# Attention's value products, two units to a PSUM bank in place of one, with 18 buffers for the turned numerators in place of 12

## The chip, the cores and the metric

The kernel runs on one core of one Trainium2 chip. The metric is the device time of one execution in microseconds (us). A difference of 0.5% of it is some 3.3 us.

## What is computed

Clustered attention on `q`, `k`, `v` of shape (2, 8, 768, 64), then two mixing layers (`_moe_ref` and `_moe2_ref`) on the (2, 768, 512) result. The change lies in the attention:

```python
scores = scale * np.matmul(q, k.transpose(0, 1, 3, 2))
scores = np.where(mask, scores, -1000000000.0)
scores = scores - np.max(scores, axis=-1, keepdims=True)
attn = np.exp(scores)
attn = attn / (np.sum(attn, axis=-1, keepdims=True) + 1e-09)
return np.matmul(attn, v)
```

## The kernel before

The attention is cut into 48 **units**, one per batch b, head h and third u of the queries (256 of 768). A name such as `s062` means batch 0, head 6, query tile 2 (a unit has the query tiles 2u and 2u+1); two heads are a **pair**, six units. Each unit passes three stages on PE (TensorE):

- `scores` (L381): for each of its two query tiles, four matmuls of 384 columns (L398, L399) into a tile `s` of two PSUM banks. Pool `ps_s` has two such tiles. DVE (VectorE) takes the negated row maximum `nm` (L401), ACT (ScalarE) the exponential `e` with its row sums (L403). Only then may the tile be written again, by the scores two query tiles later.
- `turn` (L410): twelve transposes of `e` (L418) into three PSUM tiles `t` of one bank (pool `ps_t`, three tiles, which the masks' products and `natural` use too). Each is copied to an SBUF tile `p`: two of the three by ACT (L421), the third by DVE (L423). There are `PB` buffers of tag `p`.
- `values` (L427): the products of the turned numerators with `v` (L439). Even and odd key tiles go to the two 64-column halves of the array (`tile_position=(0, r)`), into one half of the PSUM bank `o` (pool `ps_o`, one bank). Then ACT copies the upper 64 partitions to `tmp` (L446), and DVE adds the lower 64 to it, into `xt` (L448).

The loop over the units (L486) is skewed: step n traces the scores of unit n, the transposes of unit n-1 and the values of unit n-2 (`SKEW`). `values` takes a list of `GROUP` units: all their products first, then all their evacuations.

```python
group.append((n - SKEW, prs.pop(n - SKEW), ops[b, h][4]))
if len(group) == GROUP:
    with tc.issue_after(marks["turn"].ins):
        values(group)
    group = []
```

Once a pair, masks for a later pair are made (products `sim` into 32-column strips of the array at L247, a product `pp` at L271, the rest on DVE), and `natural` (L452) transposes a finished pair (L461) and divides by the row sums (DVE, L463). The order of each engine's instructions is set by the compiler's list scheduler from this program; at run time each engine runs its list in order and waits on semaphores. After the attention, from about 240 us on, the mixing layers run on PE nearly without a pause; weights are loaded and split for them on ACT, DVE and POOL (L104 to L117, L81 to L87).

Of the kernel before, what the change touches and what calls it, by code (L numbers as in the profile page):

```python
# [25 lines left out]

KINDS = "AAV"

GROUP = 1
PB = 12  # L30
RAW = 4
HL = 4

# [17 lines left out]
def tile_model(ctx: ExitStack, tc: tile.TileContext, qT, kT, v, cent, w1, w2, wc1, wc2, wth, wri, wch, out):  # L51
# [110 lines left out]
    with ExitStack() as actx:  # L162
# [247 lines left out]
        def turn(b, h, u, es):  # L410

            pr = []
            for j in range(NT // 2):
                ps = ps_t.tile([P, 2, 256], F32, tag="t", name=f"t{b}{h}{u}{j}")
                for i in range(2):
                    for a in range(2):
                        kt = 2 * j + a
                        marks["turn"] = nc.tensor.transpose(ps[:, a, i * P : i * P + P], es[i][:, kt * P : kt * P + P], ident)  # L418
                p = ap.tile([P, 2, 256], F32, tag="p", bufs=PB, name=f"p{b}{h}{u}{j}")
                if KINDS[j] == "A":  # L420
# [65 lines left out]
        for n in range(len(units) + SKEW):  # L486
# [42 lines left out]
            if 0 <= n - SKEW:  # L529
                b, h, u = units[n - SKEW]  # L530
# [3 lines that stand above are left out]
# [273 lines left out]
```

## Time and profile before

| what | value |
|---|---|
| time, median of 3 runs | 660.72 us (660.63 to 663.01) |
| the profiled execution: its time | 661.38 us |
| its span | 659.5 us (1.9 us lie around it) |
| granted TensorE clock, mean | 0.995 of full |
| busy: PE, PE's weight loads, DVE, ACT, POOL | 98%, 78%, 61%, 52%, 39% |

A profile row gives the line, the engine, the operation, the tiles (out<-in) and how often. In a timeline the first number is the start in us, the second the time covered; matmuls are pipelined, so that the distance from one start to the next is what a matmul costs, not its length. "[0.62 <-ACT e L403]" says that the engine sat idle for 0.62 us and that L403 of ACT ended it. A 32-bit matmul of L439 stands twice in the trace, so that a unit's six products are twelve records.

### The profile page before, as it was taken

How to read it: one execution, taken by the hardware profiler on the slowest of the kernel's cores; microseconds unless marked ns; L12 is line 12 of the kernel's file. 1: busy time of each engine (PE TensorE's matmuls, PEld its weight loads, DVE VectorE, ACT ScalarE, POOL GpSimd, SP SyncE). 2: the span in 40 equal slices, each digit the busy share in tenths (PEclk: the TensorE clock that was granted, in tenths of full speed). 3: DMA queues.
4: the chain of work that ended last, by engine and by line, in shares of the span. 5: the costliest groups of instructions: out<-in, count | busy, mean ns of one | idle time of the engine just before them, and what ended most of it. 6: DMA issues, size and time to landing. Idle time of an engine off the chain costs nothing. (4 is left out here: it accounts for less than half of the span.)

```text
span 659.5 us, 9798 instructions
## 1 busy us (share of the span) xinstructions
PE 645.3 (98%) x3591; PEld 517.3 (78%) x3591; DVE 399.9 (61%) x649; ACT 344.5 (52%) x653; POOL 258.4 (39%) x231
## 2 busy tenths in 40 slices
PE   7999999999999999999999999999999999999998
PEld 4777777777777767878888878888888888888886
DVE  6777878687777777466655432537577875431212
ACT  6676766776768763256544520427486954320000
POOL 7230303255031131138786520602467698541000
PEclk8999999999999999999999999999999999999999
DMA  8554656454454221013444321210022224410001
GB/s 297 158 125 110 169 122 159 102 135 101 109 132 108 66 73 64 24 64 128 133 155 128 97 64 32 68 62 0 1 64 65 72 88 144 125 50 33 16 33 48
DMA packets 24207, 61.42 MB, mean 93 GB/s; under 512 B 4256, under 2 KB 7520, under 8 KB 24160
## 3 DMA queue, kind: packets, MB, share of 16 engines
q1 hardware_dynamic: 24160, 60.80, 32.8%
q8 instruction: 28, 0.46, 0.3%
q14 instruction: 19, 0.16, 0.1%
HBM read 39.65 MB, written 3.15 MB: 65 GB/s over the span
## 5 line engine op out<-in xcount | busy, mean ns | idle before, releaser
L401 DVE TENSOR_REDUCE nm<-s 128x1 f32<-128x768 f32 x96 | 90.5, 950 | 20.1 <-PE s L399 19.2
L403 ACT ACTIVATE e<-s,nm 128x768 f32<-128x768 f32 x96 | 86.6, 905 | 29.4 <-DVE nm L401 28.1
L418 PE MATMUL t<-ident,e 128*128 128x128 f32 x576 | 81.2, 276 | 0.6 <-ACT p L421 0.5
L418 PEld LDWEIGHTS t<-ident,e 128*128 128x128 f32 x576 | 67.0, 141 | 16.3 <-issue 9.4
L398 PE MATMUL s<-k,qh 128*128 128x384 f32 x188 | 72.3, 385 | 2.4 <-ACT e L403 2.3
L439 PE MATMUL o<-p,vs 128*64 128x256 f32 x564 | 71.2, 388 | 0.0
L399 PE MATMUL s<-k,q 128*128 128x384 f32 x192 | 65.7, 345 | 1.9 <-DVE q L280 1.9
L421 ACT ACTIVATE p<-t 128x512 f32<-128x512 f32 x96 | 52.2, 594 | 25.8 <-PE t L418 25.4
L127 PE MATMUL r<-ul,c_h 128*128 128x512 f32 x144 | 56.5, 396 | 0.4 <-DVE ul L91 0.4
L128 PE MATMUL c<-c_h,rl 128*128 128x512 f32 x144 | 55.8, 390 | 0.8 <-DVE rl L645 0.8
L127 PE MATMUL y<-zl,k_h 128*128 128x512 f32 x144 | 56.2, 390 | 0.0
L129 PE MATMUL y<-zh,k_h 128*128 128x512 f32 x144 | 56.1, 389 | 0.0
L128 PE MATMUL r<-uh,c_l 128*128 128x512 f32 x144 | 56.1, 389 | 0.0
L128 PE MATMUL y<-zh,k_l 128*128 128x512 f32 x144 | 56.0, 389 | 0.0
L129 PE MATMUL r<-uh,c_h 128*128 128x512 f32 x144 | 56.0, 390 | 0.0
L129 PE MATMUL c<-c_h,rh 128*128 128x512 f32 x144 | 55.8, 390 | 0.0
L127 PE MATMUL c<-c_l,rh 128*128 128x512 f32 x144 | 55.3, 392 | 0.0
L439 PEld LDWEIGHTS o<-p,vs 128*64 128x64 f32 x564 | 36.3, 136 | 22.7 <-issue 5.5
L117 POOL TENSOR_TENSOR c_f<-c_f,c_raw 128x512 uint32<-128x512 uint32 x24 | 31.6, 1319 | 44.4 <-issue 26.2
L81 POOL TENSOR_SCALAR qh<-ql 128x768 fp32r<-128x768 f32 x7 | 5.8, 836 | 101.0 <-DMA qh<-qh 100.9
L398 PEld LDWEIGHTS s<-k,qh 128*128 128x128 f32 x188 | 35.6, 190 | 10.8 <-ACT e L403 5.3
L399 PEld LDWEIGHTS s<-k,q 128*128 128x128 f32 x192 | 37.0, 194 | 3.8 <-ACT k L277 3.4
(192 smaller groups left out, 1383.9 us busy)
## 6 DMA issues: line engine op xcount, KB each, us to landing
c_raw<-wc SPq DMA_DIRECT2D x24, 512.0 KB, 3.3
k_raw<-wri SPq DMA_DIRECT2D x18, 512.0 KB, 3.6
qh<-qh SPq DMA_DIRECT2D x28, 192.0 KB, 3.0
k<-kh SPq DMA_DIRECT2D x28, 192.0 KB, 3.9
ql<-qT SPq DMA_DIRECT2D x8, 384.0 KB, 3.2
kl<-kT SPq DMA_DIRECT2D x8, 384.0 KB, 4.2
vs<-v SPq DMA_DIRECT2D x16, 192.0 KB, 2.4
w_raw<-w SPq DMA_DIRECT2D x6, 512.0 KB, 4.2
```

The source lines that it names most:

```text
L81: nc.gpsimd.tensor_scalar(out=h, in0=x, scalar1=1.0, scalar2=0.0, op0=ALU.mult, op1=ALU.add)
L117: nc.gpsimd.tensor_tensor(out=wu, in0=wu, in1=lo, op=ALU.add)
L127: nc.tensor.matmul(ps, ah, bl, start=first and i == 0, stop=False)
L128: nc.tensor.matmul(ps, al, bh, start=False, stop=False)
L129: nc.tensor.matmul(ps, ah, bh, start=False, stop=last and i == n - 1)
L398: nc.tensor.matmul(ps[:, half, :NH], qh[:, c], k1[:, n], start=True, stop=False)
L399: marks["scores"] = nc.tensor.matmul(ps[:, half, :NH], ql[:, c], kk[:, n], start=False, stop=True)
L401: marks["max"] = nc.vector.tensor_reduce(out=nm, in_=ps[:, :, :NH], axis=AX.XY, op=ALU.max, negate=True)
L403: marks["exp"] = nc.scalar.activation(out=e.rearrange("p (a n) -> p a n", a=2), in_=ps[:, :, :NH], func=AF.Exp, bias=nm, accum_out=sums[b, ...
L418: marks["turn"] = nc.tensor.transpose(ps[:, a, i * P : i * P + P], es[i][:, kt * P : kt * P + P], ident)
L421: marks["pA"] = nc.scalar.activation(out=p, in_=ps, func=AF.Copy)
L439: nc.tensor.matmul(po[r : r + 64, :], vs[:, kt, :], pr[kt // 2][:, kt % 2, :], start=kt < 2, stop=kt >= NT - 2, tile_position=(0, r),)
```

## The change

`GROUP` goes from 1 to 2: `values` is called for every second unit, with two units, whose products fill the two halves of one `o` bank back to back. `PB` goes from 12 to 18. Nothing else is edited; the scheduler makes a new order.

```diff
-GROUP = 1
-PB = 12
+GROUP = 2
+PB = 18
```

PE, the end of head 6 and start of head 7 of batch 0, before (`t0612` are transposes, `o18` the values of unit 18, `s070` the first scores of head 7, `x02.` those of `natural`):

```order
L418 MATMUL t0612_1465<-ident_61,e063_1387 128x128 x2
L439 MATMUL o18_1472<-p0600_1403,vs06_1211 64x256 x2
L439 MATMUL o18_1472<-p0601_1410,vs06_1211 64x256 x2
L439 MATMUL o18_1472<-p0602_1417,vs06_1211 64x256 x2
L398 MATMUL s070_1499<-k107_1314,qh07_1313 128x384
L399 MATMUL s070_1499<-k2_1_152,q2_1_150 128x384
L398 MATMUL s070_1499<-k107_1314,qh07_1313 128x384
L399 MATMUL s070_1499<-k2_1_152,q2_1_150 128x384
L461 MATMUL x020_1485<-ident_61,xt04_921 128x128 x4
```

With the change, the same place:

```order
L418 MATMUL t0612_1456<-ident_61,e063_1369 128x128 x2
L398 MATMUL s070_1480<-k107_1306,qh07_1305 128x384
L399 MATMUL s070_1480<-k2_1_152,q2_1_150 128x384
L398 MATMUL s070_1480<-k107_1306,qh07_1305 128x384
L399 MATMUL s070_1480<-k2_1_152,q2_1_150 128x384
L461 MATMUL x020_1466<-ident_61,xt04_916 128x128 x4
L461 MATMUL x024_1475<-ident_61,xt04_916 128x128 x2
L271 LDWEIGHTS ltri_140
L271 MATMUL pp10_1499<-eqT10_1440,ltri_140 128x384
L398 MATMUL s071_1489<-k107_1306,qh07_1305 128x384
```

The block of values that stood between the transposes and `s070` is gone from here.

PE, a little later, with the change (`t0622` and `t0700` are transposes of units 20 and 21):

```order
L418 MATMUL t0622_1518<-ident_61,e065_1436 128x128 x2
L439 MATMUL o18_1525<-p0600_1385,vs06_1204 64x256 x2
L439 MATMUL o18_1525<-p0601_1392,vs06_1204 64x256 x2
L439 MATMUL o18_1525<-p0602_1399,vs06_1204 64x256 x2
L439 MATMUL o18_1525<-p0610_1447,vs06_1204 64x256 x2
L439 MATMUL o18_1525<-p0611_1454,vs06_1204 64x256 x2
L439 MATMUL o18_1525<-p0612_1461,vs06_1204 64x256 x2
L418 MATMUL t0700_1576<-ident_61,e070_1487 128x128 x2
```

The products of units 18 and 19 now stand in one block, behind `s071` and `s072`.

ACT at the same place, before (`tmp052` empties the bank of unit 17, `tmp060` that of unit 18, `e` are exponentials, `p` copies of transposes):

```order
L446 ACTIVATE tmp052_1426<-o17_1419 64x256 [waits PE_49,Activation_49]
L403 ACTIVATE e064_1436,sm06_1293<-s064_1429,nm064_1434 128x768 [waits DVE_49,Activation_49]
L421 ACTIVATE p0610_1456<-t0610_1451 128x512 [waits PE_49]
L421 ACTIVATE p0611_1463<-t0611_1458 128x512 [waits PE_49]
L403 ACTIVATE e065_1445,sm06_1293<-s065_1438,nm065_1443 128x768 [waits DVE_49,Activation_49]
L446 ACTIVATE tmp060_1479<-o18_1472 64x256 [waits PE_49,Activation_49]
L403 ACTIVATE e070_1506,sm06_1293<-s070_1499,nm070_1504 128x768 [waits DVE_49,Activation_49]
```

With the change:

```order
L446 ACTIVATE tmp051_1414<-o16_1401 64x256 [waits PE_49,Activation_49]
L446 ACTIVATE tmp052_1417<-o16_1401 64x256 [waits DVE_49]
L403 ACTIVATE e064_1427,sm06_1285<-s064_1420,nm064_1425 128x768 [waits DVE_49,Activation_49]
L421 ACTIVATE p0610_1447<-t0610_1442 128x512 [waits PE_49]
L421 ACTIVATE p0611_1454<-t0611_1449 128x512 [waits PE_49]
L403 ACTIVATE e065_1436,sm06_1285<-s065_1429,nm065_1434 128x768 [waits DVE_49,Activation_49]
L403 ACTIVATE e070_1487,sm06_1285<-s070_1480,nm070_1485 128x768 [waits DVE_49,Activation_49]
```

Two evacuations now follow each other, the second waiting for DVE's use of the first, and none stands between `e065` and `e070`.

## Rows read from the trace of the kernel before

**Rows 1.** the page's part 1: busy time, share of the span, instructions.
```profile
PE 645.3 (98%) x3591; PEld 517.3 (78%) x3591; DVE 399.9 (61%) x649; ACT 344.5 (52%) x653; POOL 258.4 (39%) x231
```

**Rows 2.** timeline of PE, one unit: start us, us, instruction, count.
```profile
154.04 0.34 PE L399 MATMUL s<-k,q 128*128 128x384 f32 x1
154.22 0.82 PE L418 MATMUL t<-ident,e 128*128 128x128 f32 x6
154.96 1.51 PE L439 MATMUL o<-p,vs 128*64 128x256 f32 x12
156.41 0.44 PE L398 MATMUL s<-k,qh 128*128 128x384 f32 x1
156.69 0.34 PE L399 MATMUL s<-k,q 128*128 128x384 f32 x1
```

**Rows 3.** costliest groups: count | busy us, mean ns of one | idle before, what ended it.
```profile
L403 ACT ACTIVATE e<-s,nm 128x768 f32<-128x768 f32 x96 | 86.6, 905 | 29.4 <-DVE nm L401 28.1
```

**Rows 4.** timeline, 109.8 to 117 us, one ring of scores, and a wait.
```profile
109.89 0.44 PE L398 MATMUL s<-k,qh 128*128 128x384 f32 x1
...
110.89 0.96 DVE L401 TENSOR_REDUCE nm<-s 128x1 f32<-128x768 f32 x1 [1.65 <-PE s L399]
...
111.94 0.90 ACT L403 ACTIVATE e<-s,nm 128x768 f32<-128x768 f32 x1 [0.89 <-DVE nm L401]
112.03 0.33 PE L399 MATMUL s<-k,q 128*128 128x384 f32 x1
112.10 1.26 DVE L463 TENSOR_TENSOR xn<-x,ri 128x128 f32<-128x128 f32 x6
...
112.99 0.44 PE L398 MATMUL s<-k,qh 128*128 128x384 f32 x1 [0.62 <-ACT e L403]
...
113.27 0.34 PE L399 MATMUL s<-k,q 128*128 128x384 f32 x1
...
113.75 1.80 DVE L401 TENSOR_REDUCE nm<-s 128x1 f32<-128x768 f32 x2
113.81 1.47 PE L418 MATMUL t<-ident,e 128*128 128x128 f32 x12
114.44 1.08 ACT L421 ACTIVATE p<-t 128x512 f32<-128x512 f32 x2 [1.50 <-PE t L418]
...
115.41 0.91 ACT L403 ACTIVATE e<-s,nm 128x768 f32<-128x768 f32 x1
...
116.29 0.91 ACT L403 ACTIVATE e<-s,nm 128x768 f32<-128x768 f32 x1
```

**Rows 5.** timeline of PE: the same place two pairs of heads earlier.
```profile
56.83 0.44 PE L398 MATMUL s<-k,qh 128*128 128x384 f32 x1 [0.62 <-ACT e L403]
```

**Rows 6.** timeline of PE: first scores of units 6 and 42; behind unit 45's values.
```profile
39.70 0.44 PE L398 MATMUL s<-k,qh 128*128 128x384 f32 x1
...
208.22 0.44 PE L398 MATMUL s<-k,qh 128*128 128x384 f32 x1
...
237.18 0.33 PE L418 MATMUL t<-ident,e 128*128 128x128 f32 x1
```

**Rows 7.** timeline, 242 to 249 us: eight records of L439, and a later wait.
```profile
242.32 1.08 PE L439 MATMUL olast<-p,vs 128*64 128x256 f32 x8
...
248.96 0.50 PE L127 MATMUL g<-xl,w_h 128*128 128x512 f32 x1 [2.58 <-DVE gl L149]
```

**Rows 8.** timeline: a block's evacuation (the block ends before 152.06).
```profile
152.06 0.44 PE L398 MATMUL s<-k,qh 128*128 128x384 f32 x1
...
152.23 0.38 ACT L446 ACTIVATE tmp<-o 64x256 f32<-64x256 f32 x1 [0.20 <-PE o L439]
...
152.65 0.42 DVE L448 TENSOR_TENSOR xt<-o,tmp 64x256 f32<-64x256 f32 x1
```

**Rows 9.** timeline, 24 to 26 us: the first values' block; the exponential of `s005`.
```profile
24.52 1.52 PE L439 MATMUL o<-p,vs 128*64 128x256 f32 x12
...
25.27 0.91 ACT L403 ACTIVATE e<-s,nm 128x768 f32<-128x768 f32 x1
```

## The prediction

> **What bounds the kernel now.** I read the page's busy times first: PE is busy 98% of the span, the others at most 61% [rows 1]. That share doesn't say yet that PE is the limit in the attention, because a matmul's length overlaps the next one. So I read the timeline of one unit by its start-to-start distances [rows 2]. There the reader sees no hole: scores, transposes and values follow each other, and ACT instead sits idle for the row maxima (28.1 us in all) [rows 3]. PE bounds the attention, with one exception: in every second pair of heads the scores wait 0.62 us for an exponential [rows 4, 5], because a scores tile comes free only after maximum and exponential. This ring is what I follow below. From the first scores of unit 6 (39.70) to those of unit 42 (208.22) six pairs pass [rows 6], 28.09 us each; from wait to wait, 56.83 to 112.99 [rows 4, 5], it is 28.08.
>
> **What the change takes away.** The price of one values' block on PE comes out of four distances.
> - Inside it: twelve records cover 1.51 us and eight cover 1.08 [rows 2, 7], so four cost 0.43 and a unit's twelve 1.29. From the block's start to the next scores it is 1.45 [rows 2]: 0.16 too much.
> - Into it: six transposes cost 0.65 (twelve cover 1.47 [rows 4], six 0.82 [rows 2], so 0.108 each), but the block starts 0.74 after them: 0.09.
> - Out of it: the first scores matmul takes 0.28, others some 0.175 [rows 2]: 0.105.
>
> Together 0.35 us for a block, at each change between 128 and 64 columns. With two units to a block there are 24 fewer: three to a pair of heads, 1.05 us. In every second pair, one block before stands next to the 32-column products of L247, which leave the 128 columns anyway; I take off 0.08 on average: **minus 0.97 us a pair**. The old wait also goes, since its place in the order is another: from 112.03 to 112.99 is 0.96 in place of 0.175, and the first step after it is again 0.28 [rows 4], 0.89 in all, every second pair: **minus 0.44**. The 18 buffers cost nothing: no copy of a transpose waits for one now, and a unit's three copies stay alive for one unit longer at most, for which six buffers more are enough.
>
> **What it puts in their place.** A block covered the ring: while PE did values, maximum and exponential ran. With two blocks in one, every second step has no cover. The ring's time is in one stretch [rows 4]: scores start at 109.89 behind a block, maximum 1.00 later, exponential 2.05 later, the next scores in that tile 3.10 later. I lay the printed order on it, with z as the start of the first scores behind a block, and a tile of scores at 0.70 (0.80 behind a block or a wait). Five places of a pair come out late:
> - **A**, `s062`: PE has 0.80 + 0.65 + 0.70 + 0.65 = 2.80 of work before it, the ring needs 3.10. Wait 0.30, restart 0.105: 0.41.
> - **B**, `s070`: 0.80 + 0.43 + 0.70 + 0.87 = 2.80 again: 0.41.
> - **C**, `s071`: on ACT stand `e064` (from z + 2.05, 0.88 from one to the next), two copies (0.97 together) and `e065` (0.90) [rows 4], so 4.80, and scores 0.15 later as in the stretch: 4.95. PE has 3.10 + 0.80 for `s070`, 0.65 for `natural` and some 0.17 for `pp`: 4.72. Wait 0.23 and restart: 0.33.
> - **D**, the transposes behind `s071`: their tile is read by `natural`'s divisions. Maximum of `s070` at 4.10, 0.85 of DVE for it (two cover 1.80, one 0.96), four divisions at 0.2 (six in 1.26): the last ends at 5.84. PE is there at 5.75: with the restart some 0.2.
> - **E**, `s075`, behind the second block: evacuation by ACT 0.17 after the block, the addition 0.42 later, for 0.42 [rows 8]; the second evacuation waits for it and ends at 1.5. Then two copies from 1.6 on and `e073` until 3.47, scores at 3.62. PE has 3.40 of work: 0.32.
>
> Sum **plus 1.67**, so a pair costs 28.08 - 0.97 - 0.44 + 1.67 = 28.34, and six pairs 1.6 us more than now. The prices of A and B are rows alone. For C to E the order of a queue decides, which no row of before shows. Their bounds: nothing, if the engine got there early (minus 0.85 a pair), and at the most the whole 0.89 of the old wait at each in place of 0.85 together (plus 1.8 a pair). I take the walked values, near the low end, since each is made of durations in the rows.
>
> **Head and tail.** Until unit 6 two blocks go (minus 0.70). But the first block, which started at 24.52, no longer covers the exponential of `s005`, which runs from 25.27 to 26.18 [rows 9]. `s011` needs that tile; with `s010` in the block's place PE asks for it at about 25.2 and gets it at 26.3: plus 1.2. Head: plus 0.5, between minus 0.7 (no wait) and plus 1.4 (a second wait of the old size). From unit 42 to the end there are no masks' products. PE's work from there to the end of the block of units 44 and 45 is twelve tiles of scores (8.4), six units' transposes (7.8), three double blocks (8.8) and `natural` (0.65), 25.65; the same walk finds waits of 1.9 in it (A and B, 0.49 at `s163`, which the masks' products no longer cover, 0.26 at C, 0.32 at E), so 27.55. Now it is 28.96 to the end of unit 45's block [rows 6], with four transposes (0.43) of later work done: minus 1.0. Behind this, PE waits 2.58 us for a subtraction of DVE [rows 7], which stands behind the splits of the weights on POOL and DVE. That chain starts from the same evacuations and swallows most of what PE brings or loses: I take minus 0.5, between minus 1 and plus 1. After it the layers are the same program on a PE without holes. DMAs: those of the next heads keep their place in SP's queue, apart from the loads of `v`, which move one or two places back and are due some 10 us later: nothing.
>
> **Sum**: 0.5 + 1.6 - 1.0 - 0.5 = +0.6 us. The profiled execution took 661.38 us (span 659.5), so 662.0 by it; the median of the runs is 0.66 lower, so **661.3 us** for runs like those. A measurement of this kernel can tell about 0.5% (3.3 us) from no change, so this is no change.
>
> **Rivals.**
> - *PE alone decides.* None of the waits comes: eight pairs at minus 0.97 make 653.0 us. For it: PE at 98%, and no other engine above 61%. Against it: 3.10 against 2.80 at A and B, and the old wait of the same kind. The Trainium skill, page "TensorEngine Tiling (Array Packing)", section "Key Properties", says that changing the tiling mode drains TensorE; by that rule alone the sum would be this rival's. The trace agrees that a change costs something, 0.35 us a block. Chance 0.05.
> - *Only A and B come.* C to E are early enough: minus 0.97, minus 0.44, plus 0.82, eight times: minus 4.7, so 656.0 us. For it: each of the three misses by 0.25 us or less. Chance 0.08.
> - *Evacuation ahead of the maximum* (slower). Behind each block, DVE now has two additions and ACT two evacuations in a chain. If the addition of the first (from z + 0.59, DVE taken for 0.35) is pushed past z + 1.00 by other work of DVE, the maximum and with it the ring at A and B slip by up to 0.33 each; it decides from a delay of 0.07 on. Two such slips a pair make 8 x 0.66 = 5.3: 666.0 us. For it: the second evacuation waits for DVE in the order. Against it: the order puts the second addition behind the maximum. Chance 0.17.
> - That the change doesn't do what it says, that is, that the scheduler takes the blocks apart, has no chance: the order shows two units to each block, but for the last.
>
> **How the numbers follow.** The forecast has 0.70, faster 0.05 + 0.08 = 0.13, slower 0.17. The range goes from 657.8 (one wait of C to E missing in most pairs, and halfway to the second rival) to 664.8 (a wait of 0.5 more in each pair); some 0.1 lies on either side.
>
> **What would show it.** In the profile after, PE should wait for ACT's L403 at two to four scores a pair, not at one in two pairs; six pairs should take 170 us, 1.6 more than 168.5; the idle time of PE in front of L398 should be some 7 to 10 us. L439 should stand in runs of 24 records. If six pairs took under 167, the ring would have been covered by something that I don't see, and the forecast would be wrong; over 172.5, ACT or DVE would have become the limit.

## The result, and where the time went

The changed kernel takes **667.6 us** (median of 4 runs, 666.79 to 668.59) beside 660.69 for the kernel before; the ratio is 1.009, 95% interval 1.0062 to 1.0118. It is slower, by 4 to 8 us, and the time lies above the range of the prediction (657.8 to 664.8). The profiled execution took 667.41 with a span of 665.3, which is 5.8 more than the span before.

The page of the changed kernel: busy times, the granted clock in 40 slices, and the scores' first matmuls (count | busy us, mean ns of one | idle before, what ended it).

```profile
PE 646.7 (97%) x3591; PEld 520.1 (78%) x3591; DVE 399.7 (60%) x649; ACT 343.3 (52%) x653; POOL 258.1 (39%) x231
...
PEclk9999999999999998999999989999999999999999
...
L398 PE MATMUL s<-k,qh 128*128 128x384 f32 x188 | 72.4, 385 | 4.8 <-ACT e L403 3.5
```

The busy times hardly differ from [rows 1]: no engine got more work. New are two slices with an 8 in the clock (the 16th, 249 to 266 us, and the 24th, 383 to 399). Four rows of PE's timeline, laid beside [rows 6, 7], cut the 5.8 us into stages.

```profile
38.88 0.45 PE L398 MATMUL s<-k,qh 128*128 128x384 f32 x1
...
209.71 0.44 PE L398 MATMUL s<-k,qh 128*128 128x384 f32 x1
...
237.54 0.44 PE L418 MATMUL t<-ident,e 128*128 128x128 f32 x2
...
250.22 0.79 PE L127 MATMUL g<-xl,w_h 128*128 128x512 f32 x1 [1.34 <-DVE gl L149]
```

| stage | before | after | difference | forecast |
|---|---|---|---|---|
| to the first scores of unit 6 | 39.70 | 38.88 | -0.8 | +0.5 |
| six pairs, to unit 42 | 168.52 | 170.83 | +2.3 | +1.6 |
| to the end of unit 45's block | 28.96 | 27.83 | -1.1 | -1.4 |
| to the second half of `g0` | 11.78 | 12.68 | +0.9 | -0.1 |
| layers, to the end of the span | 410.5 | 415.1 | +4.5 | 0 |

The prediction has -1.0 and -0.5 for the third and fourth stage, because it counts 0.43 us for four transposes in the fourth that the change does there (twelve from 237.54 on) and the kernel before ahead of it (eight from 237.18 on). The rows count them where they run, and so does the table: -1.4 and -0.1. From unit 42 to the second half of `g0` the change is 0.2 us shorter in all, where 1.5 was forecast.

The attention went about as walked. What was missed lies behind it: in the tail, and above all in layers whose program I took for unchanged.

**One pair of heads.** PE in the change, from one block to the third after it (start us, us, instruction, count):

```profile
95.81 0.45 PE L398 MATMUL s<-k,qh 128*128 128x384 f32 x1
...
96.62 0.82 PE L418 MATMUL t<-ident,e 128*128 128x128 f32 x6
97.20 0.42 PE L398 MATMUL s<-k,qh 128*128 128x384 f32 x1
97.46 0.33 PE L399 MATMUL s<-k,q 128*128 128x384 f32 x1
...
97.98 0.82 PE L418 MATMUL t<-ident,e 128*128 128x128 f32 x6
98.86 0.44 PE L398 MATMUL s<-k,qh 128*128 128x384 f32 x1
...
107.42 1.03 PE L418 MATMUL t<-ident,e 128*128 128x128 f32 x8
108.59 0.44 PE L398 MATMUL s<-k,qh 128*128 128x384 f32 x1
...
110.06 0.33 PE L271 MATMUL pp<-eqT,ltri 128*128 128x384 bf16 x1
110.45 0.45 PE L398 MATMUL s<-k,qh 128*128 128x384 f32 x1
...
111.08 0.34 PE L399 MATMUL s<-k,q 128*128 128x384 f32 x1
111.50 0.63 PE L418 MATMUL t<-ident,e 128*128 128x128 f32 x4
...
119.14 0.99 PE L418 MATMUL t<-ident,e 128*128 128x128 f32 x6
120.00 0.44 PE L398 MATMUL s<-k,qh 128*128 128x384 f32 x1
...
121.55 2.81 PE L439 MATMUL o<-p,vs 128*64 128x256 f32 x24
124.29 0.44 PE L398 MATMUL s<-k,qh 128*128 128x384 f32 x1
```

All five waits of the prediction are there. Six transposes and a step into scores take 0.58 us where nothing waits (96.62 to 97.20). At A they take 0.88 (97.98 to 98.86), at E 0.86 (119.14 to 120.00); at B eight take 1.17 (107.42 to 108.59), 0.38 more than 0.58 and two steps of 0.108. At C the scores start 0.39 behind `pp`, where the kernel before has 0.03 in its steps from `pp` to scores; at D the transposes start 0.42 behind the last scores matmul, where 0.17 is usual. I count 0.02 more for the restart at A, B, C and E, since the first scores matmul behind a wait takes 0.28 and behind transposes without a wait 0.26. That is 0.32 + 0.40 + 0.38 + 0.25 + 0.30 = 1.65 us a pair, beside a forecast of 1.67. At A, B and C the profile names L403 as what ended the wait. At E some 0.18 of it stands in front of the last two transposes, which wait for a copy of DVE, and the rest in front of the scores. The page shows only 4.8 us of idle time in front of L398, because it counts from a matmul's modelled end; distances of starts tell more.

**The tail.** DVE and PE where units 46 and 47 are evacuated:

```profile
245.21 0.42 DVE L448 TENSOR_TENSOR xt<-olast,tmp 64x256 f32<-64x256 f32 x1 [1.18 <-ACT tmp L446]
...
246.18 1.69 DVE L87 TENSOR_TENSOR w_l<-w_f,w_h 128x512 fp32r<-128x512 f32 x2 [0.55 <-POOL w_h L81]
...
247.90 0.42 DVE L448 TENSOR_TENSOR xt<-olast,tmp 64x256 f32<-64x256 f32 x1
...
248.47 0.41 PE L461 MATMUL x<-ident,xt 128*128 128x128 f32 x2 [1.56 <-DVE xt L448]
```

The first addition runs at 245.21. The second, whose `tmp` was there at 246.0, stands in DVE's list behind two splits of weights (1.69 us). So PE waits 1.56 us for `xt`, and then 1.34 for `gl`, in place of one wait of 2.58 [rows 7], and starts the second half of `g0` 0.9 us later, counted from unit 45's block. Then the clock: the columns of these windows are PE, its weight loads, DVE, ACT and POOL busy, granted clock, DMA share, GB/s.

```profile
248.00:250.00 2.00, 0.41 (x2) 0.20 (x2) 1.97 (x7) 0.59 (x1) 0.00 (x0) 1.00 0.09 33
250.00:252.00 2.00, 1.78 (x4) 1.49 (x5) 1.16 (x4) 0.63 (x1) 0.61 (x1) 0.54 0.00 0
252.00:254.00 2.00, 2.00 (x7) 1.52 (x6) 0.57 (x1) 1.02 (x2) 1.31 (x2) 0.60 0.18 31
```

Behind a stretch in which PE was busy for 0.41 of 2 us, the granted clock is at its lower level (1.2 GHz) for some 3 us, and the steps of the 512-column matmuls rise from 0.23 to 0.43. From 250.2 to 254 the distance to before grows by another 1.55 us.

**The layers.** PE waits a second time at 388, and the clock falls again (the last row is a window with the columns above):

```profile
388.20 0.47 PE L127 MATMUL c<-c_l,rh 128*128 128x512 f32 x1 [1.41 <-ACT rh L644]
389.48 0.49 PE L128 MATMUL c<-c_h,rl 128*128 128x512 f32 x1 [0.81 <-DVE rl L645]
```

```profile
390.00:392.00 2.00, 2.00 (x6) 1.58 (x6) 0.03 (x1) 0.00 (x0) 1.44 (x2) 0.53 0.38 98
```

Before, at 384.04, the same matmul waits for 0.03 us and only the second wait (0.81) is there:

```profile
384.04 0.47 PE L127 MATMUL c<-c_l,rh 128*128 128x512 f32 x1
385.32 0.51 PE L128 MATMUL c<-c_h,rl 128*128 128x512 f32 x1 [0.81 <-DVE rl L645]
```

The longer wait adds 1.4 us to the distance to before, the low clock behind it 1.6. What is late is a rectifier on ACT that stands behind the split of a theta weight, which waits for its transfer:

```profile
386.36 0.67 ACT L111 ACTIVATE th_raw<-th_raw 128x512 uint32<-128x512 uint32 x1 [3.48 <-DMA th_raw<-wth]
...
387.46 1.09 ACT L644 ACTIVATE rh<-r 128x512 fp32r<-128x512 f32 x2
```

From 296 us on the loads are a chain (a raw buffer comes free, 512 KB are loaded, and split on ACT, DVE and POOL). From the first product `r` to the third `th_raw` it takes 99.6 us before and 101.0 here, while PE's way to the matmul that wants it is the same 101.4. Before and change, the issue of two loads and the split that waits for the first:

```profile
294.04 2.33 SPq L104 DMA_DIRECT2D c_raw<-wc  x2
...
297.55 0.67 ACT L111 ACTIVATE c_raw<-c_raw 128x512 uint32<-128x512 uint32 x1 [0.17 <-DMA c_raw<-wc]
```

```profile
296.87 2.31 SPq L104 DMA_DIRECT2D c_raw<-wc  x2
...
302.29 0.67 ACT L111 ACTIVATE c_raw<-c_raw 128x512 uint32<-128x512 uint32 x1 [2.12 <-DMA c_raw<-wc]
```

The split starts 3.5 us after the issue before, and 5.4 in the change.

### The profile page after: what moved, and what is told of

Its sections match the earlier page's. It is cut to its first block, busy times and chain, and to the rows that moved or that the text cites. A ratio compares the mean times of both kernels' runs of the same rounds, so it can differ in the third digit from the quotient of the medians.

```text
span 665.3 us, 9777 instructions
## 1 busy us (share of the span) xinstructions
PE 646.7 (97%) x3591; PEld 520.1 (78%) x3591; DVE 399.7 (60%) x649; ACT 343.3 (52%) x653; POOL 258.1 (39%) x231
## 5 line engine op out<-in xcount | busy, mean ns | idle before, releaser
L403 ACT ACTIVATE e<-s,nm 128x768 f32<-128x768 f32 x96 | 86.7, 904 | 20.4 <-DVE nm L401 20.3
L398 PE MATMUL s<-k,qh 128*128 128x384 f32 x188 | 72.4, 385 | 4.8 <-ACT e L403 3.5
L399 PE MATMUL s<-k,q 128*128 128x384 f32 x192 | 64.3, 337 | 1.9 <-DVE q L280 1.9
L439 PE MATMUL o<-p,vs 128*64 128x256 f32 x552 | 64.6, 383 | 0.0
L439 PEld LDWEIGHTS o<-p,vs 128*64 128x64 f32 x552 | 37.6, 137 | 20.5 <-issue 3.9
L398 PEld LDWEIGHTS s<-k,qh 128*128 128x128 f32 x188 | 35.4, 188 | 17.6 <-ACT e L403 11.5
L652 DVE TENSOR_TENSOR xn<-c,xn 128x512 f32<-128x512 f32 x36 | 24.3, 685 | 25.9 <-PE c L129 25.9
```

The lines of the kernel that those rows point to most:

```text
L398: nc.tensor.matmul(ps[:, half, :NH], qh[:, c], k1[:, n], start=True, stop=False)
L399: marks["scores"] = nc.tensor.matmul(ps[:, half, :NH], ql[:, c], kk[:, n], start=False, stop=True)
L403: marks["exp"] = nc.scalar.activation(out=e.rearrange("p (a n) -> p a n", a=2), in_=ps[:, :, :NH], func=AF.Exp, bias=nm, accum_out=sums[b, ...
L439: nc.tensor.matmul(po[r : r + 64, :], vs[:, kt, :], pr[kt // 2][:, kt % 2, :], start=kt < 2, stop=kt >= NT - 2, tile_position=(0, r),)
L652: nc.vector.tensor_tensor(out=xn[t], in0=ps, in1=xn[t], op=ALU.add)
```

## Experiments

Three theories went in. END: the attention costs little, the loss comes from the tail (units 46 and 47 together), the clock behind it and the late weights. RING: the attention's waits are the cause of all. CHANCE: the late weights belong to the one profiled execution. All times are medians beside the kernel before on the same chip, with the ratio and its 95% interval. The ratio is no quotient of the two medians, so that a price differs by up to 1 us with the one that it is read from; where it matters, the text says which.

**The change again, its two constants and its tail apart.** The first run is the changed kernel unedited, the second has `PB = 18` alone. The third and the fourth edit one line:

```diff
-                if len(group) == GROUP:
+                if len(group) == GROUP or n - SKEW >= len(units) - 4:
```

```diff
-                if len(group) == GROUP:
+                if len(group) == (2 if n - SKEW >= len(units) - 2 else 1):
```

> The changed kernel once more, unedited. Three theories of its 6.9 us. END: the attention costs only some 1.5 us up to the last pair; the rest comes behind it, from the last two units (46 and 47) being evacuated together (a wait of 1.26 us more in front of the second half of g0, then about 1.55 us at the lower TensorE clock), and from weights that come late at 388 us (1.36 us more, and 1.6 us at the lower clock). RING: the waits in the attention are the cause, and what is seen in the layers only follows from PE being elsewhere in time. CHANCE: the late weights (one transfer of 512 KB that took 5.31 us in place of 3.41) belong to the one execution that was profiled. END and RING expect 667.4 +- 1 and the same two stretches at about 0.55 of the clock; CHANCE expects a transfer of 3.4 us at the same place, no wait at 388, and 664.5 for this execution.

> GROUP stays 1, PB goes to 18: the buffers alone. END, RING and CHANCE all expect 660.7 +- 0.5 and the same trace as before; a gain or a loss of over 1 us would show that the place of the buffers matters, which none of them has.

> GROUP 2 and PB 18, but units 44 to 47 each in a block of their own, so that the tail's order is that of before. END: first scores of unit 42 some 1.5 us later than before as with the change, then the wait for gl swallows this, full clock at 250, no wait at 388: 661 +- 1. RING: the six pairs cost the same as with the change, so the time stays at 666 to 668. CHANCE: as END, or 1 to 3 us more if a transfer of the weights happens to be late.

> GROUP 1 and PB 18, but units 46 and 47 in one block: the attention of before with the tail of the change. END: the second half of g0 starts 1.0 to 1.3 us later and the clock is lower behind it for some 3 us: 663.5 if the late weights do not come with it, 666.5 if they do. RING: 660.7. CHANCE: 663.5 in most executions.

Measured, with before at 662.33: 667.12 (ratio 1.0071, 1.0044 to 1.0098) for the repetition, 661.89 (1.000, 0.9979 to 1.0021) for the buffers alone, 664.5 (1.0044, 1.0025 to 1.0064) with the last four apart, 663.99 (1.0023, 1.0010 to 1.0036) with the last two together. So the buffers are worth nothing; by the ratios, doubled blocks cost 2.9 us without the changed tail (2.2 by the medians), and the tail alone 1.5 (1.7). In the trace of the fourth run, unit 42's scores and the second half of `g0` lie 41.97 us apart in place of 40.74, so that this tail costs 1.2 us by itself, and the clock is low behind it (columns as above):

```profile
250.00:252.00 2.00, 2.00 (x6) 1.54 (x6) 0.73 (x3) 1.17 (x2) 1.20 (x2) 0.55 0.15 29
```

RING falls: in the third run the attention is as slow as in the change (six pairs 170.9 us), and the time is 664.5, not 666 to 668. CHANCE falls: in the repetition the split again starts 5.4 us after the issue, the waits at 388 are 1.52 and 0.82, and the clock is low at 252. END was right on the parts and wrong on one: for the third run I expected the wait for `gl` to swallow what the attention lost (661). It stays 2.58 long in the third run, whose span is 3.6 over before: the chain of weights starts from the same evacuations and moves with them.

**Filling the waits at 248.** Matmuls that nobody reads (`marks["xt"]` is the transpose of L461 traced last):

```diff
+                if (b, pr) == (1, H // 2 - 1):
+                    if q0 == 0:
+                        fps = ps_t.tile([P, 4, P], F32, tag="t", name="fill")
+                    with tc.issue_after(marks["xt"].ins):
+                        for i in range(14 if q0 == 0 else 12):
+                            nc.tensor.transpose(fps[:, i % 4, :], ident, ident)
```

> The changed kernel, with matmuls that nobody reads (14 and 12 transposes of the identity into a free PSUM tile) in the two places near 248 us where PE waits 1.56 and 1.34 us. END: the waits stay as long, but PE is busy in them, the granted clock stays full at 250, and the time falls by 1.3 to 1.7 us from 667.1 to some 665.6; the late weights at 388 and what they bring stay. CHANCE (the lower clock comes anyway, whatever PE did before): about 0.55 at 250 again, 667.

Measured 665.01 beside 661.95 (1.0047, 1.0028 to 1.0066): 3.1 us over before, where the unedited change has 4.8 in the repetition. PE, then two windows as above:

```profile
247.81 1.69 PE L467 MATMUL fill<-ident 128*128 128x128 f32 x14
249.54 0.41 PE L461 MATMUL x<-ident,xt 128*128 128x128 f32 x2
249.78 1.47 PE L467 MATMUL fill<-ident 128*128 128x128 f32 x12
251.29 0.50 PE L127 MATMUL g<-xl,w_h 128*128 128x512 f32 x1
```

```profile
250.00:252.00 2.00, 1.96 (x15) 1.64 (x14) 2.00 (x7) 0.17 (x1) 0.00 (x0) 1.00 0.00 0
252.00:254.00 2.00, 2.00 (x11) 1.61 (x10) 0.24 (x2) 1.82 (x4) 1.84 (x2) 1.00 0.00 0
```

The same waits, filled, and the clock stays full. The two intervals overlap, so the times alone don't settle what the fill gives back; in the profiled executions the distance to before grows by some 0.55 us from the second half of `g0` to 280 us, in place of 1.55. The waits at 388 (1.50 and 0.81) are still there, as END said. In this execution the load at 297 us lands after 3.2 us; several of the later ones take 4.0 to 4.4.

**The blocks in another place.** Unit 0 alone, then units 1 and 2, and so on. Unit 47 is left over in this kernel, and its value products are left out.

```diff
-                if len(group) == GROUP:
+                if len(group) == GROUP or n == SKEW:
```

> GROUP 2 and PB 18, but unit 0 in a block of its own, so that blocks hold units 1 and 2, 3 and 4, ... 45 and 46, and 47 stands alone. RING PRICE: every second step is without cover as in the change, only at other places; four or five waits a pair again, six pairs 169.5 to 171.5. If the place matters (the masks' products or natural would now stand where PE waited), six pairs come under 168.5 and this is the better version. Tail: 47 alone, so one addition fewer behind the weights' splits, the waits near 248 between those of before and of the change. Time 662 to 667.

Measured 667.91 (1.0075, 1.0045 to 1.0105), with less work. Six pairs take 175.7 us, 7.2 more than before and above the 169.5 to 171.5 expected, and once in each pair of heads transposes wait 0.69 us for a copy of ACT. So the place matters, and the change has the better one of the two.

**Without the ring.** The first two runs let the exponential take a constant zero as its bias; the maximum is computed and not used.

> The kernel before (GROUP 1, PB 12), with the row maximum still computed by DVE but not used: the exponential takes a constant zero as its bias (this leaves the subtraction of the maximum out). The order of every matmul stays. It takes the 0.95 us of the maximum out of the ring of a scores tile, 3.10 down to about 2.15, under the 2.80 of PE's work. RING PRICE (the waits for L403 make the difference between the two kernels in the attention): the wait of every second pair goes, six pairs take 168.5 - 6 x 0.44 = 165.9, the time is some 657. NO RING (the doubled blocks themselves cost PE time): nothing changes but the old wait, the same 165.9.

> The changed kernel with the same edit (the maximum computed, not used; the subtraction left out). RING PRICE: no score waits any more, PE alone decides, and three values' blocks fewer a pair are worth 0.97: six pairs take 160.0, 5.8 less than in the kernel before with the same edit; the tail and the layers lose what they lost, so the time is some 656. NO RING: six pairs stay above those of the kernel before with the same edit, 166 to 168. In between (a saving of less than 0.35 us a block): 161 to 165, and the price of a block is then the difference divided by 18.

They tell nothing on the ring. The exponential still starts when DVE's maximum ends, although it no longer uses it (what makes it wait, no run shows):

```profile
112.02 0.90 ACT L403 ACTIVATE e<-s,nm 128x768 f32<-128x768 f32 x1 [0.89 <-DVE nm L401]
```

Six pairs take 168.5 and 170.8 as ever. The times rose to 670.67 and 672.95, all of it in the layers (see the last section). The next two leave the maximum out altogether.

> The kernel before without the row maximum (left out, as is its subtraction: the exponential takes a constant zero as its bias). In the two runs with an unused maximum the exponential still waited for it, so that the ring was as long as ever; here it is really gone. The scheduler's order changes a little. RING PRICE: no score waits; six pairs 165.9 (168.5 less 6 x 0.44). NO RING: 165.9 too.

> The changed kernel without the row maximum, as in the run beside it (maximum and subtraction left out). RING PRICE: no score waits, six pairs 160.0, about 6 us less than the run beside it: eighteen blocks fewer at 0.35 us. NO RING (a doubled block is no saving): 166 or more. In between: the difference over 18 is the price of a block.

They took 664.09 and 663.97 us, one execution each. Six pairs took 165.2 us with single blocks, near the 165.9 forecast for a gone ring, but 164.1 with doubled ones, not 160.0: 1.1 us for eighteen blocks, 0.06 each. That is not the block's price: without the maximum the scheduler gives both kernels another order, and with doubled blocks scores still start late in it, as behind `pp`:

```profile
107.39 0.33 PE L271 MATMUL pp<-eqT,ltri 128*128 128x384 bf16 x1
107.71 0.44 PE L398 MATMUL s<-k,qh 128*128 128x384 f32 x1
```

The pair is inconclusive. The price is better read from before and change as they are: a pair of the change without its 1.65 us of waits takes 28.47 - 1.65 = 26.82, one of before without the old wait 28.09 - 0.44 = 27.65. That is 0.83 us for three blocks, 0.28 each. It is a difference of sums, no experiment: what the waits are misread by goes into it.

**The late weights: more buffers, or another order.** First a fourth raw buffer (`bufs=4` of tag `wraw`, `NBLK = 49`, and `PB = 16` in the change):

> The changed kernel with four buffers in place of three for the raw weights (PB 16 and NBLK 49 to make room). END, as mended by the first runs: in the layers the loads of the weights run as a chain (a buffer comes free, 512 KB are loaded, split on ACT, DVE and POOL), and from the first product r to the third th_raw it takes 98.5 to 101.1 us while PE needs 101.4 to the product that wants it some 1.8 us later: no slack, so every late transfer shows at 388. With one buffer more the chain has slack: no wait at 388 (now 1.4 to 1.5 and 0.8), none of the lower clock behind it, 667 falls by 2.2 to 3.5, to 664 +- 1. If the chain is bound by something else (ACT's order), the waits stay and so does 667.

> The kernel before with four buffers for the raw weights (NBLK 49; PB 12). The chain's slack: the wait of 0.81 at 385 goes, and the executions in which a transfer is late lose nothing: some 1 us less than before, 660.5 to 661.5 beside a before of 662. If the chain is bound by something else: the same as before.

Measured, with before at 661.94: 667.4 (1.0093, 1.0072 to 1.0113) and 663.44 (1.0026, 1.0010 to 1.0042). It doesn't help; the kernel before is a little slower with it. In the changed kernel the third `th_raw` is split 5 us earlier, 95.9 after the first `r`, but the scheduler uses the room to put the split of the fourth one ahead of the same `rh`:

```profile
389.65 0.65 ACT L111 ACTIVATE th_raw<-th_raw 128x512 uint32<-128x512 uint32 x1 [3.66 <-DMA th_raw<-wth]
...
390.76 1.06 ACT L644 ACTIVATE rh<-r 128x512 fp32r<-128x512 f32 x2
```

So it is ACT's order, and the next edit changes that (`rh` marks the last rectifier of the block before):

```diff
-            wt = [load_w(wth[:, c * 512 : c * 512 + 512], f"th_{c}") for c in range(NC)]
+            with tc.issue_after(rh.ins):
+                wt = [load_w(wth[:, c * 512 : c * 512 + 512], f"th_{c}") for c in range(NC)]
```

> The changed kernel, with the four loads of the theta weights issued behind the last rectifier rh of the block before, so that no split of a theta weight (L111, L110) stands ahead of an rh on ACT. The run with four raw buffers showed that more buffers do not help, because the scheduler then puts the split of the next weight there. END: the waits at 388 (1.41 and 0.81) go, and with them what the lower clock costs behind them in some executions: 667.1 falls by 2.2 to 3, to 664.5 +- 0.7. If the matmul at 388 waits for something else, or if the later loads only move the wait (theta's products at 450), 667 stays.

> The kernel before with the same edit. END: its wait at 385 (0.81 in the profiled execution, none in that with 18 buffers) goes: 0.4 to 0.9 us less than before on the same chip. If the gain of the run beside it is 2 us more than this one's, the change and not the kernel before paid for the late weights.

> Doubled blocks but for units 44 to 47, with the same edit: the attention's part of the loss alone, with the tail of before and nothing late at 388. END: 0 to 0.8 under the 664.5 of the run without the edit, that is, some 2 us over before on the same chip: six pairs 2.3 us longer, nothing given back. RING as the cause of everything: 666 or more.

> The changed kernel with both edits (unread matmuls in the two waits near 248, theta weights later). END: the parts add up: 667.1 less 2.1 for the fill and 2.2 for the weights, 662.8 +- 0.7; what is left over before on the same chip (about 1) is the attention and the longer wait at 248. If the two share a cause, the gain is less than the sum: 664 to 665.

Measured, with before at 660.93: 665.64 for the change (1.0071, 1.0047 to 1.0096), 660.47 for the kernel before (0.999, 0.9976 to 1.0005), 663.96 with the last four apart (1.0052, 1.0035 to 1.0068), 662.93 with the fill (1.0040, 1.0026 to 1.0054). No wait is left at 388 in any of the four. But the first gained next to nothing on the repetition (both ratios are 1.0071), and its granted clock was low for twice as long behind the tail (2.8 us lost there in place of 1.55; mean 0.990 in two of four executions). So this edit ran once more beside the unedited change.

> The changed kernel unedited, beside the next run on one chip, so that the theta weights' price is read from two kernels that share their runs of before. END: 1.007 to 1.009 of before, with waits of some 1.4 and 0.8 at 388.

> The changed kernel with the theta weights issued later, as in the earlier run of this edit, whose trace had no wait at 388 but whose time was only 0.9 us nearer to before than the changed kernel's on other chips. If the waits at 388 cost what the trace shows (2.2 us, less about 0.8 that before pays too), it is 1.4 to 2.2 us under the run beside it; if the lower clock takes it back in most executions, 0 to 1 us.

Measured 666.46 (1.0062, 1.0044 to 1.0079) and 663.91 (1.0040, 1.0025 to 1.0056), before at 661.62. The late weights cost the changed kernel 2.55 us by the medians and 1.5 by the ratios, so about the 1.4 to 2.2 expected; the executions of either kernel lie 2.6 to 4.4 us apart, and no closer price can be had. In the profiled execution of the unedited kernel, the clock was low at 390 for some 3 us as well. At 250 it stayed full there, but PE lost 1.34 us a little later all the same, to a subtraction that stands in DVE's list behind five others (3.1 us):

```profile
258.72 0.50 PE L127 MATMUL h<-gl,w_h 128*128 128x512 f32 x1 [1.18 <-DVE gl L149]
```

So the low clock behind the tail hides a wait that partly comes in its place when the clock stays full. With the edit, ACT has the rectifier first:

```profile
385.35 0.58 ACT L644 ACTIVATE rh<-r 128x512 fp32r<-128x512 f32 x1
...
386.39 1.80 ACT L111 ACTIVATE th_raw<-th_raw 128x512 uint32<-128x512 uint32 x3
```

The parts add up within their intervals, which reach 0.9 to 1.8 us to either side. By the ratios, doubled blocks with the tail of before cost 2.9 to 3.4 us (1.0044 and 1.0052), the tail 1.5 and the late weights 1.5; the full change stood at 1.0062, 1.0071 and 1.0090, 4.1 to 5.9 us. The change with both edits behind the attention is at 1.0040, 2.6 us: attention, and a tail 0.2 us shorter on PE. The version that does best is the kernel before with the theta weights later, 0.5 us under before; its interval includes no change.

## Why the prediction was wrong, step by step

- **The five waits** (plus 1.67 a pair): right, each in its place, 1.65 by the rows above.
- **The price of a block** (minus 0.97 a pair): 0.83. The step that was too large is "out of it": I charged 0.105 for the first scores matmul behind a block, but behind transposes it is slow too (0.26, 97.20 to 97.46, beside 0.28). That leaves 0.265 a block and 0.80 for three, near 0.83 without the 0.08 that I took off for the products of L247. With 0.83 the six pairs come to +2.3 in place of +1.6. They are steady: 170.8 to 171.0 us in the eleven profiled executions with blocks doubled as in the change and the maximum computed, 168.5 in six with single blocks. The Trainium skill, page "TensorEngine Tiling (Array Packing)", section "Key Properties", says that changing the tiling mode drains TensorE; the 0.28 us a block agree that the change of columns has a price, and by that rule alone (653.0) the forecast would have been further off. The idle time in front of L398, which I put at 7 to 10 us as a sign, came to 4.8.
- **The head** (plus 0.5): the profiled execution shows -0.8, but this moves with the first transfers. Over the same eleven executions the first scores of unit 6 start at 39.97 in the mean (38.88 to 41.11), over the six at 39.44 (38.71 to 40.39): +0.5, less than they scatter. Counted from the first scores of unit 2, behind the first transfers, it is 18.99 to 19.30 us with single blocks and 19.54 to 20.14 with doubled ones, +0.7 in the mean: about right.
- **The tail to unit 45's block** (minus 1.0, with the four transposes set off): -0.7 in these terms, so 0.3 too much.
- **"I take minus 0.5"** for the wait in front of `g0`, since the chain of weights "swallows most of what PE brings or loses": this step failed, twice. The chain starts from the evacuations and so moves with PE; it swallows nothing (the wait is 2.58 again with the last four apart). And I looked only at PE's order there. In DVE's order the second addition of units 46 and 47 stands behind 1.69 us of splits; the stage came to +0.9 in place of the -0.1 that the forecast comes to in these rows, and this tail alone gives +1.2 in the kernel before.
- **"After it the layers are the same program on a PE without holes"**: this failed most: I put the layers at nothing, and they took 3.1 to 4.5 us more in three profiled executions. That a program is the same doesn't make its time the same. Its loads had no slack against PE (a wait of 0.03 at 384.04 before), so transfers that came later became waits of 1.0 to 1.5 us. And long waits of PE can be followed by some 3 us at the lower clock, which cost 1.3 to 1.6 us each time here.
- **The rival on the slower side** (666.0) came near the measured time by another way: the additions of DVE did delay something, not the maxima behind each block but the last transposes. That it came near is luck.

The cause is settled in its parts, with one thing open: what makes the chain of loads late by the 1.4 us that show at 388. The load at 297 us takes 5.1 to 5.4 us (from issue to split) in three executions of the changed kernel and 3.5 before, but it isn't needed for it: with the waits filled it landed after 3.2, and the wait at 388 was 1.50 all the same. A load of 16 KB of instructions falls into the same stretch in the change and before. It wasn't tried by itself.

## What to carry to other kernels

Where a change shortens or lengthens one stage, look in every queue at the joint to the next stage, not in the bound engine's alone: DVE's order at the end of the attention, with the low clock behind it, and ACT's order in the layers held the larger part of the loss. A stage that "stays the same" has a price when a transfer or a weight arrives there with no slack; look in its rows for waits of nearly nothing. And a long wait on TensorE is to be costed with the lower clock that may follow it; if the wait can't be removed, matmuls into a free bank can keep the clock up, as in both kernels here that filled theirs.

## What the runs showed of the hardware that I had not expected

- **The clock after waits inside a kernel.** Behind PE's waits of 1.56 and 1.34 us it was low in two of three profiled executions of the change, behind one wait of 2.58 not in that of the kernel before, but in that with 18 buffers. Over all kernels with either tail it fell in seven of eight profiled executions behind the two waits, in three of seven behind the one wait, and in neither of the two with filled waits. So a wait makes the fall likely and doesn't decide it; what does is open. The times follow: with 18 buffers the two executions whose mean clock was 1.000 took 660.0 and 660.1 us, the four at 0.992 took 662.7 to 664.4. The Trainium skill, page "TensorE: Matmul & The Clock Gate", section "Part 1: The HAM clock gate", says that the throttled state is the default and that activity releases it. The windows above agree, 0.54 behind the two waits and 1.00 where unread matmuls filled them.
- **Where a weight begins in SBUF.** The four kernels that replace or drop the maximum have one small tile more or fewer, and in the compiled programs all weights then begin 32 bytes past a multiple of 64. The 512-column matmuls of the layers take 0.233 to 0.234 us from start to start there (median from 300 us on) and 0.227 in all others, at the same granted clock of 1.00: some 8 us by the end. PE in the kernel before with the unused maximum:

```profile
299.98 0.39 PE L129 MATMUL r<-uh,c_h 128*128 128x512 f32 x1
...
300.91 0.63 PE L127 MATMUL r<-ul,c_h 128*128 128x512 f32 x2
```

From 299.98 to 300.91 there are four steps (the three rows left out are such matmuls too); they take 0.93; at 0.227 they would take 0.91. The address was not varied by itself.
